# Moving two kinds of matmul operands by 32 bytes in SBUF

## The chip, the cores and the metric

The kernel runs on one core of a Trainium2 chip. The metric is the time of one execution on the device in microseconds (us), as the median of several runs. Engines are called as in the profile: PE is TensorE (matmuls), PEld its weight loads, DVE VectorE, ACT ScalarE, POOL GpSimd, SP the engine whose queue issues all transfers. A matmul has a stationary operand (128x128, loaded beforehand by an instruction of its own) and a moving operand (128 partitions by 256 or 512 columns here), and writes to PSUM.

## What is computed

Causal attention with decay, whose output goes through two feed-forward blocks. Cut to what matters:

```python
scores = (q @ k.T) / sqrt(64) * where(i >= j, gamma[h] ** (i - j), 0)   # 8 x 8 heads, 576 positions
x = (scores @ v)                                  # as 4608 tokens x 512
h = maximum(maximum(x @ w1, x @ w2), x @ w3)      # 768 wide
x = h @ w_out                                     # 512 wide
a, b = x @ w1, x @ w2                             # second block, 1024 wide
x = (a * b @ w3) @ w_out                          # 512 wide
```

The products need float32 accuracy: each operand is split into a high and a low part of the type float32r (`xh`, `xl`), and a product is made of three: high by high, low stationary by high moving, high stationary by low moving.

## The kernel before

There are five stages of matmuls, in this order of time.

- **First product** (`products`, L476), with the attention of later tokens between its groups (L335 to L402). Blocks of 512 tokens; for each of 6 row blocks `f` and 3 weights `i`, 12 matmuls of 512 columns go into one PSUM bank `ps_h`. Stationary: `w1h`, `w1l`, from the pool `w1`. Moving: `xh`, `xl`, from the pools `x0`, `x1`, `x2`. The first matmuls of all are cut in halves of 256 columns.
- **Product z** (the loop over `z_groups`, banks `ps_X`, `ps_V`, `ps_Y`), a Strassen form with 7 products a group: 4 groups of 512 columns (126 matmuls each) and one of 256. Stationary: the sums `za11h` to `zs4l`; moving: the ring `hh`, `hl`. Both from the pool `zp`.
- **Product of w3 and w_out** (`ps_w`): 192 matmuls of 512 columns. Stationary: `th`, `tl`; moving: `oh`, `ol`; both from the pool `t34`, which also has the landing tiles `raw34`.
- **Gate product** (the loop over `visits`, banks `ps_x`, `ps_v`, `ps_y`): ten visits, eight with 512 columns (168 matmuls each) and two, next to each other, with 256. Stationary: `a..`, `s..` in pieces of the pool `ws` and two of the pool `wk`. Moving: one of two operand sets in turn, `ops[0]` in the pool `op0` and `ops[1]` in the pool `op1`.
- **Last product** (`add_o`), 18 steps `s` of 84 matmuls of 256 columns. Stationary: `a11h` to `s4l`, made by `g_steps(s)` in `gpool[s % 2]`: the pool `ga` for even steps and `gb` for odd ones. Moving: tiles `k..` of the pool `ga` and pieces `w..` of the pool `ws`. The matmuls run in the order of the program; the first two products of step s + 1 (`a11`, `a12`) run ahead of the last one of step s (`a22`).

All of them are issued by two lines, L476 and L705 (`product`), so the rows of the trace are told apart by tile names. All transfers are issued by SP in program order (`load`, L100).

**Where the tiles lie.** Pools have a side. Those of the left are stacked upwards from the bottom of SBUF: the first tile lies at byte 640 of each partition, which is a multiple of 64, and all tiles ahead of the matmul operands are multiples of 256 bytes, so every operand on the left (`w1`, `x0` to `x2`, `t34`, `ws`, `wk`, `op1`, `ga`) begins at a multiple of 64. Those of the right are stacked downwards from byte 229,344, which is 64 x 3583 + 32; their tiles are multiples of 64 too, so every operand on the right (`zp`, `op0`, `gb`, and the attention's pools) begins 32 past a multiple of 64. In a pool on the right a tile that is made later lies above the earlier ones and moves the pool's start down, so that the earlier tiles move down by its size, and the later ones don't.

The remainders by 64, as (moving, stationary): first product (0, 0); z (32, 32); product of w3 and w_out (0, 0); gate product (32, 0) with `ops[0]` and (0, 0) with `ops[1]`; last product (0, 0) in even steps and (0, 32) in odd ones.

Of the kernel before, what the change touches and what calls it, by code (L numbers as in the profile page):

```python
# [9 lines left out]
F32 = mybir.dt.float32  # L10
# [12 lines left out]
P = 128  # L23
# [65 lines left out]
def tile_retention_maxout_bilinear(ctx: ExitStack, tc, a, out):  # L89
# [3 lines left out]
    def copy_r(dst, src):  # L93
        nc.scalar.activation(dst, src, AF.Copy)  # L94

    def low(eng, dst, full, hi):
        eng.tensor_tensor(dst, full, hi.bitcast(F32), ALU.subtract)  # L97

    def load(dst, src):
        nc.sync.dma_start(out=dst, in_=src)  # L100
# [14 lines left out]
        return ps_mm.tile([P, 512], F32, tag="mm", name=name)  # L115

    left = ctx.enter_context(ExitStack())
    hb_p = left.enter_context(tc.tile_pool(name="hb", bufs=4, side="left"))
    w1_p = left.enter_context(tc.tile_pool(name="w1", bufs=1, side="left"))
    x_p = {2: left.enter_context(tc.tile_pool(name="x2", bufs=1, side="left"))}  # L120
    cv_x = ctx.enter_context(ExitStack())
    x_p.update({t: cv_x.enter_context(tc.tile_pool(name=f"x{t}", bufs=1, side="left")) for t in range(2)})
    cv = cv_x.enter_context(tc.tile_pool(name="cv", bufs=2, side="left"))
    right = ctx.enter_context(ExitStack())
# [367 lines left out]
    for t in range(n_blk):  # L492
        for f in range(KF1):
            for i in range(3):
                k = T_BLK * t + 3 * f + i
                if t < EARLY:
                    split = t == 0 and 3 * f + i < HALVED
                    for e, cols in enumerate(halves if split else (whole,)):
                        name = f"{t}.{3 * f + i}" + "ab"[e] * split
# [20 lines left out]
    def splitter(pool, src, hi, lo, eng, tag, bufs):  # L520
        raw = pool.tile([P, hi.shape[-1]], F32, tag=tag, name=tag, bufs=bufs)
        load(raw, src)

        def split():
            copy_r(hi, raw)
            low(eng, lo, raw, hi)

        return split

    def open_z():  # L530
        right.close()
        cv_x.close()
        zp["ps"] = ctx.enter_context(tc.tile_pool(name="ps_2", bufs=2, space=PSUM, side="right"))
        p = zp["p"] = bx.enter_context(tc.tile_pool(name="zp", bufs=1, side="right"))
        zp["w"] = {x: [p.tile([P, KH, half], F32R, name=f"z{x}{v}") for v in "hl"] for x in AN}

    def raw_h(tag, bufs=1):
        return zp["p"].tile([P, KH, N1], F32, tag=tag, name=tag, bufs=bufs)
# [64 lines left out]

    t_last = T_BLK * (n_blk - 1)
    when(t_last, open_z)
    for c, tag in enumerate(("T3", "T2", "b21")):
        for n, step in enumerate(z_weights(c, tag)):
# [11 lines left out]
    with tc.manual_schedule():  # L619
# [88 lines left out]
        t34, w3t, wo2 = {}, {}, {}  # L708
# [4 lines left out]
            return splitter(t34["p"], flat(w3t_d[:, k, 4 * e:4 * e + 4]), *map(flat, w3t[n]), nc.vector, "raw34", 3)  # L713

        def get_wo2(k):
            wo2[k] = [t34["p"].tile([P, DM], F32R, tag=x, name=x) for x in ("oh", "ol")]
            return splitter(t34["p"], wo2_d[:, k], *wo2[k], nc.gpsimd if k % 2 else nc.vector, "raw34", 3)

# [2 lines left out]
        def prepare_34(*gets):  # L721
            for split in pending:
                split()
            pending[:] = [get(n) for get, n in gets]

        first_34 = [((get_w3t, 0), (get_wo2, 0)), ((get_w3t, 1),), ((get_w3t, 2), (get_wo2, 1)), ()]

        def open_34():
            t34["p"] = t34x.enter_context(tc.tile_pool(name="t34", bufs=2, side="left"))

        zo_p = bx.enter_context(tc.tile_pool(name="zo", bufs=1, side="right"))

# [16 lines left out]
        for j, (_, _, _, size) in enumerate(z_groups):  # L749
# [25 lines left out]
            if j == 3:  # L775
                for step in steps:
                    step()
                sx.close()
                open_34()
                steps = [lambda gets=gets: prepare_34(*gets) for gets in first_34]  # L780
# [6 lines left out]
        def operand_set(pool, tag):  # L787
            return {x: [pool.tile([P, 2, N1], F32R, name=f"{x}{v}{tag}") for v in "hl"] for x in BN}

        ops = [operand_set(o_p, 0)]  # L790
        behind = []

        def lows():
            for fn in behind:
                fn()
            behind.clear()


        def raw_z():
            return zr_p.tile([P, 2, 2, N1], F32, tag="zr", name="zr")  # L800
# [71 lines left out]
        for n in range(2 * KF2):  # L872
            k, e = divmod(n, 2)
            th, tl = w3t.pop(n)
            for m in range(4 * e, 4 * e + 4):
                if k == 0:
                    ps_w.append(bank8(f"ps_w{m}"))
                product(ps_w[m], [(th[:, m % 4], tl[:, m % 4], *wo2[k])], k == 0, k == KF2 - 1)
                if k == KF2 - 1:
                    t = w4_p.tile([P, DM], F32, tag="w4", name="w4")  # L880
                    copy_r(t, ps_w[m])
                    load(w4_d[:, m], t)
            prepare_34(*[(get_w3t, n + 3)] * (n + 3 < 2 * KF2), *[(get_wo2, k + 2)] * (e == 1 and k + 2 < KF2))
            lows()
            if steps:
                steps.pop(0)()
# [68 lines left out]
        gpool, last, gq = [None, None], {}, {}  # L955

        def temp():
            return spare_z()
# [48 lines left out]
        def g_steps(s):  # L1007

            w, ops = {}, gq.setdefault(s, {})

            def fetch():

                lows()
                r = raw_z().rearrange("p a b (c e t) -> p (a b c) e t", c=2, e=2)
                blk, e = divmod(turn[s], 2)
                load(r.rearrange("p k e t -> p k (e t)"), g_d[blk][:, :, 2 * P * e:2 * P * e + 2 * P])
                for e in range(2):
                    for kk in range(2):
                        w[f"a{e + 1}{kk + 1}"] = r[:, 4 * kk:4 * kk + 4, e]

            def split(x, eng):
                h, l = ops[x] = [gpool[s % 2].tile([P, 4, P], F32R, tag=f"{x}{v}", name=f"{x}{v}") for v in "hl"]
                src = w[x]
                copy_r(h, src)
                if s:
                    low(eng, l, src, h)
                else:
                    behind.append(lambda: low(eng, l, src, h))

            def add(dst, x, y, op, t):  # L1030
                nc.vector.tensor_tensor(t, w[x], w[y], op)
                w[dst] = t

            def tmp():
                return temp().rearrange("p (k t) -> p k t", k=4)

            def over(dst, x, y, op, to):
                lows()
                add(dst, x, y, op, w[to])

            if s == 0:
                return [fetch,
                        lambda: split("a11", nc.vector),
                        lambda: add("s1", "a21", "a22", ALU.add, tmp()),
                        lambda: over("s3", "a11", "a21", ALU.subtract, "a21"),
                        lambda: split("a12", nc.vector),
                        lambda: add("s2", "s1", "a11", ALU.subtract, tmp()),
                        lambda: split("s1", nc.vector),
                        lambda: split("s3", nc.vector),
                        lambda: over("s4", "a12", "s2", ALU.subtract, "a12"),  # L1050
                        lambda: split("s2", nc.vector),
                        lambda: split("a22", nc.vector),
                        lambda: split("s4", nc.vector)]
            return [fetch,
                    lambda: (split("a11", nc.gpsimd), add("s1", "a21", "a22", ALU.add, tmp())),
                    lambda: (split("a12", nc.vector), add("s2", "s1", "a11", ALU.subtract, tmp())),
                    lambda: (split("s1", nc.vector), add("s3", "a11", "a21", ALU.subtract, w["a21"])),
                    lambda: (split("s2", nc.gpsimd), add("s4", "a12", "s2", ALU.subtract, w["a12"])),
                    lambda: split("s3", nc.vector),
                    lambda: (split("s4", nc.vector), split("a22", nc.gpsimd))]  # L1060
# [218 lines left out]
```

## Time and profile before

| | us |
|---|---|
| median of 3 runs | 1280.26 |
| lowest and highest | 1279.84, 1280.35 |
| the profiled execution | 1279.71 |
| its span, first to last instruction | 1278.0 |
| PE busy in the span | 1270.4 |
| DVE, ACT, POOL busy | 884.6, 488.2, 311.5 |

The page of the profile gives busy times and the chain of work that ended last. A matmul's own duration (389 ns for 512 columns) is modelled to its last write and overlaps the next, so the pace is read from the distance between starts: the length of a stretch divided by the number of matmuls that start in it. The granted clock is 1.00 of 2.4 GHz in every stretch shown.

### The profile page before, as it was taken

The numbers are of one execution on the slowest core, as the hardware profiler recorded it, in microseconds if no ns is written. First come the engines' busy times: TensorE is split into PE (matmuls) and PEld (weight loads), VectorE is DVE, ScalarE is ACT, GpSimd is POOL, SyncE is SP. The second block draws the span as 40 slices with busy tenths as digits, with TensorE's granted clock in tenths as the row PEclk, the third lists the DMA queues.
The fourth block names the chain that finished last, engine by engine and source line by source line (L and its number), as shares of the span: only waits on it lengthen the run. The fifth ranks groups of instructions, "written<-read, shape, count | busy, mean of one in ns | idle before, by whom it ended". The sixth has DMA issues, their size and how long they took to land.

```text
span 1278.0 us, 23000 instructions
## 1 busy us (share of the span) xinstructions
PE 1270.4 (99%) x8904; PEld 1088.6 (85%) x8904; DVE 884.6 (69%) x1256; ACT 488.2 (38%) x873; POOL 311.5 (24%) x259
## 2 busy tenths in 40 slices
PE   8999999999999999999999999999999999999999
PEld 6888888888888888888889788888988888999998
DVE  5985666666666765467897547775766577888885
ACT  3550122222222222225554444443433344455553
POOL 2111211111111110000000324553345352344443
DMA  9935788788888994525544641424133323445542
GB/s 215 249 100 123 147 216 200 186 206 194 225 190 169 185 208 121 180 84 198 198 157 144 219 166 70 140 77 158 63 110 117 132 74 124 156 156 161 170 151 100
DMA packets 323797, 199.34 MB, mean 156 GB/s; under 512 B 241636, under 2 KB 279270, under 8 KB 323688
## 3 DMA queue, kind: packets, MB, share of 16 engines
q1 hardware_dynamic: 323688, 197.87, 55.8%
q8 instruction: 70, 1.15, 0.4%
q14 instruction: 39, 0.32, 0.1%
HBM read 131.76 MB, written 66.06 MB: 155 GB/s over the span
## 4 chain that ended last, share of the span: by engine, by line
PE 98%; DMA 1%; DVE 0%; ACT 0%; issue 0%; SPq 0%; POOL 0%; ACTq 0%; POOLq 0%
PE ps_h L476 35%; PE ps_x L705 24%; PE ps_y L705 12%; PE ps_v L705 6%; PE ps_X L705 6%; PE ps_Y L705 3%; PE sc L359 3%; PE o L374 3%; PE ps_w L705 2%; PE ps_V L705 1%; PE st L394 1%; PE o L381 1%; DMA raw<-w3t_d 1%; PE kp L335 0%; PE warm L260 0%; PE qp L335 0%
## 5 line engine op out<-in xcount | busy, mean ns | idle before, releaser
L476 PE MATMUL ps_h<-xh,w1h 128*128 128x512 f32 (+1 forms) x664 | 257.2, 389 | 0.0
L476 PE MATMUL ps_h<-xh,w1l 128*128 128x512 f32 (+1 forms) x664 | 254.1, 384 | 0.0
L476 PE MATMUL ps_h<-xl,w1h 128*128 128x512 f32 (+1 forms) x664 | 174.1, 384 | 0.0
L476 PEld LDWEIGHTS ps_h<-xh,w1h 128*128 128x128 f32 x664 | 124.7, 188 | 27.6 <-issue 2.1
L476 PEld LDWEIGHTS ps_h<-xh,w1l 128*128 128x128 f32 x664 | 124.8, 188 | 24.0
L476 PEld LDWEIGHTS ps_h<-xl,w1h 128*128 128x128 f32 x664 | 123.1, 188 | 24.7
L486 DVE TENSOR_TENSOR hb<-ps_h,hb 128x512 f32<-128x512 f32 (+1 forms) x110 | 74.3, 677 | 96.8 <-PE ps_h L476 85.5
L1133 POOL TENSOR_TENSOR c<-c 128x512 f32<-128x512 f32 (+1 forms) x60 | 83.5, 1392 | 181.9 <-DVE c L1125 127.9
L1120 ACT ACTIVATE snap<-ps_x 128x512 f32<-128x512 f32 (+1 forms) x100 | 55.5, 555 | 182.0 <-PE ps_x L705 169.6
L345 POOL TENSOR_TENSOR q<-q,tables 128x512 f32<-128x512 f32 (+1 forms) x31 | 31.3, 1009 | 278.7 <-DMA q<-in_q_dram 207.0
L94 ACT ACTIVATE hb<-ps_h 128x512 f32<-128x512 f32 (+1 forms) x56 | 32.5, 580 | 141.7 <-PE ps_h L476 141.7
L160 ACT ACTIVATE e<-raw 128x512 f32<-128x512 f32 x64 | 42.8, 669 | 105.3 <-DMA raw<-in_moe_w_dram 70.9
L94 ACT ACTIVATE xh<-o 128x512 fp32r<-128x512 f32 (+1 forms) x40 | 22.2, 555 | 119.9 <-PE o L381 84.3
L97 POOL TENSOR_TENSOR ol<-raw,oh 128x512 fp32r<-128x512 f32 x4 | 5.7, 1432 | 239.7 <-DVE tl L97 218.7
L348 POOL TENSOR_TENSOR v<-v,tables 128x512 f32<-128x512 f32 x40 | 43.5, 1089 | 59.3 <-DMA v<-in_v_dram 59.3
L366 DVE TENSOR_TENSOR p<-sc,mask 128x512 f32<-128x512 f32 (+1 forms) x80 | 48.1, 627 | 12.9 <-PE sc L359 12.8
L1125 DVE TENSOR_TENSOR c<-ps_x,snap 128x512 f32<-128x512 f32 (+1 forms) x40 | 25.2, 637 | 43.2 <-PE ps_x L705 31.1
L166 DVE CUSTOM_DVE_ANT_0 m<-m,r 128x1024 uint16<-128x1024 uint16 x64 | 48.6, 759 | 7.5 <-ACT r L161 0.5
L1125 DVE TENSOR_TENSOR c<-ps_v,snap 128x512 f32<-128x512 f32 (+1 forms) x40 | 25.1, 635 | 37.8 <-PE ps_v L705 20.9
L705 PE MATMUL ps_x<-t4h,a 128*128 128x512 f32 (+1 forms) x160 | 45.9, 370 | 0.3 <-DVE a L97 0.3
L705 PE MATMUL ps_x<-b11h,a 128*128 128x512 f32 (+1 forms) x160 | 45.8, 371 | 0.0
L169 DVE SCALAR_TENSOR_TENSOR m<-raw,m 128x512 int32<-128x512 int32 x64 | 45.5, 715 | 0.3
(296 smaller groups left out, 3281.0 us busy)
## 6 DMA issues: line engine op xcount, KB each, us to landing
zr<-g_d SPq DMA_DIRECT2D x18, 1024.0 KB, 6.1
raw<-in_moe_w_dram SPq DMA_DIRECT2D x34, 512.0 KB, 6.1
g_d<-c SPq DMA_DIRECT2D x64, 256.0 KB, 2.0
zr<-z_d SPq DMA_DIRECT2D x28, 512.0 KB, 5.3
h_d<-hb SPq DMA_DIRECT2D x54, 256.0 KB, 3.2
b<-h_d SPq DMA_DIRECT2D x16, 768.0 KB, 6.2
out_dram<-ob SPq DMA_DIRECT2D x35, 256.0 KB, 2.1
v<-in_v_dram SPq DMA_DIRECT2D x32, 256.0 KB, 4.4
```

The lines of the kernel that those rows point to most:

```text
L94: nc.scalar.activation(dst, src, AF.Copy)
L160: nc.scalar.activation(z["e"], raw[:, :, 1].bitcast(F32), AF.Copy, scale=2.0 ** -112)
L166: nc.vector.tensor_tensor(z["m"], z["m"], z["r"], ALU.add)
L169: nc.vector.scalar_tensor_tensor(z["m"], z["hi"], -0x80000000, z["m"], ALU.bitwise_and, ALU.bitwise_or)
L348: nc.gpsimd.tensor_tensor(z["v"], z["v"], vd.unsqueeze(2).to_broadcast([P, H, D]), ALU.mult)
L366: nc.vector.tensor_tensor(z[g][:c, :, :c], z["sc"][g][:c, :, :c], mask[:c, :c].unsqueeze(1).to_broadcast([c, G, c]), ALU.mult)
L476: nc.tensor.matmul(ps[:, cols], l, r, start=n == 0, stop=n == len(mms) - 1)
L486: nc.vector.tensor_tensor(hb, ps[:, cols], hb, ALU.max)
L705: nc.tensor.matmul(ps, l, r, start=start and j == 0, stop=stop and j == len(mms) - 1, skip_group_check=again)
L1120: nc.scalar.activation(t, ps[:, :size], AF.Copy)
L1125: nc.vector.tensor_tensor(r, ps[:, :size], t, ALU.add)
L1133: nc.gpsimd.tensor_tensor(x, x, y, ALU.mult)
```

## The change

A helper `skew` makes a tile of 32 bytes per partition (8 float32) that nothing reads or writes. It is called in seven places:

```diff
     left = ctx.enter_context(ExitStack())
+    def skew(pool, n=0):
+        pool.tile([P, 8], F32, name=f"skew{n}", bufs=1)
+
+    skew(ctx.enter_context(tc.tile_pool(name="edge", bufs=1, side="right")))
     hb_p = left.enter_context(tc.tile_pool(name="hb", bufs=4, side="left"))
     w1_p = left.enter_context(tc.tile_pool(name="w1", bufs=1, side="left"))
+    skew(w1_p)
     x_p = {2: left.enter_context(tc.tile_pool(name="x2", bufs=1, side="left"))}
+    skew(x_p[2])
...
         zp["w"] = {x: [p.tile([P, KH, half], F32R, name=f"z{x}{v}") for v in "hl"] for x in AN}
+        skew(p)
...
         def get_wo2(k):
+            if k == 0:
+                skew(t34["p"], 1)
             wo2[k] = [t34["p"].tile([P, DM], F32R, tag=x, name=x) for x in ("oh", "ol")]
...
             t34["p"] = t34x.enter_context(tc.tile_pool(name="t34", bufs=2, side="left"))
+            skew(t34["p"])
...
             def split(x, eng):
+                if not ops and s in (0, 3):
+                    skew(gpool[s % 2])
                 h, l = ops[x] = [gpool[s % 2].tile([P, 4, P], F32R, tag=f"{x}{v}", name=f"{x}{v}") for v in "hl"]
```

The pool `edge` lies at the right-hand end for the whole kernel and moves everything on the right down by 32 bytes. The first tile of `w1` moves its weights up by 32; the one in `x2` brings `xh` and `xl` of all three pools back to a multiple of 64. In `zp` the tile comes after the sums and before the ring, so the sums move by 32 more than the ring. In `t34` one tile moves `th`, `tl` and `raw34`, and a second one `oh` and `ol` back. In `ga` (s = 0) the tile comes after the moving tiles `k..` and ahead of the stationary ones; in `gb` (s = 3) it is the last tile of its pool and moves all others down.

The remainders by 64 afterwards: first product, z, product of w3 and w_out, and both kinds of steps of the last product (0, 32); gate product (0, 0) with both sets. The attention's operands move by 32 together.

## Rows read from the trace of the kernel before

**Rows 1.** The page: busy time by engine, and the chain's shares by engine.
```profile
PE 1270.4 (99%) x8904; PEld 1088.6 (85%) x8904; DVE 884.6 (69%) x1256; ACT 488.2 (38%) x873; POOL 311.5 (24%) x259
...
PE 98%; DMA 1%; DVE 0%; ACT 0%; issue 0%; SPq 0%; POOL 0%; ACTq 0%; POOLq 0%
```

**Rows 2.** Waits of PE, longest first (total, times, longest).
```profile
PE sc L359 <- DVE qt L342: 1.9, 2, 1.0
```

**Rows 3.** Busy time by stretch; columns as in the first line.
```profile
core 0: us, PE busy (x) PEld busy (x) DVE busy (x) ACT busy (x) POOL busy (x), PEclk, DMA share, GB/s
513.82:568.21 54.39, 54.39 (x241) 45.06 (x240) 29.25 (x52) 15.86 (x31) 0.00 (x0) 1.00 0.44 150
570.48:684.76 114.28, 114.28 (x505) 94.59 (x504) 96.79 (x89) 61.77 (x71) 0.00 (x0) 1.00 0.52 174
684.77:699.87 15.10, 15.10 (x127) 15.10 (x126) 10.11 (x16) 9.33 (x17) 0.00 (x0) 1.00 0.38 124
...
745.23:784.43 39.20, 39.20 (x169) 31.54 (x168) 22.15 (x26) 16.67 (x30) 17.43 (x12) 1.00 0.34 121
784.44:822.55 38.11, 38.11 (x169) 31.54 (x168) 29.14 (x36) 18.23 (x34) 18.93 (x12) 1.00 0.32 111
901.82:929.41 27.59, 27.59 (x232) 27.59 (x231) 19.77 (x39) 12.92 (x31) 7.39 (x9) 1.00 0.17 59
1018.08:1056.19 38.11, 38.11 (x169) 31.54 (x168) 24.87 (x30) 15.54 (x28) 17.58 (x12) 1.00 0.28 91
1056.20:1095.40 39.20, 39.20 (x169) 31.54 (x168) 30.30 (x42) 18.26 (x34) 9.93 (x6) 1.00 0.38 127
1110.00:1278.00 168.00, 164.96 (x1391) 164.76 (x1390) 137.24 (x178) 84.66 (x178) 70.43 (x49) 1.00 0.47 150
```

**Rows 4.** Starts of matmuls of the last product: start, duration, engine, line, what.
```profile
1138.19 0.29 PE L705 MATMUL ps_y<-kt,s1h 128*128 128x256 f32 x1
...
1143.94 0.28 PE L705 MATMUL ps_x<-kb,a11h 128*128 128x256 f32 x1
...
1148.20 0.28 PE L705 MATMUL ps_y<-kt,s1h 128*128 128x256 f32 x1
...
1153.83 0.28 PE L705 MATMUL ps_x<-kb,a11h 128*128 128x256 f32 x1
```

**Rows 5.** Groups by form: count, busy us and mean ns of one, idle before.
```profile
L476 PE MATMUL ps_h<-xh,w1h 128*128 128x512 f32 x632 | 248.7, 394 | 0.0
L476 PE MATMUL ps_h<-xh,w1l 128*128 128x512 f32 x632 | 246.2, 389 | 0.0
L476 PE MATMUL ps_h<-xl,w1h 128*128 128x512 f32 x632 | 169.0, 389 | 0.0
...
L705 PE MATMUL ps_w<-oh,th 128*128 128x512 f32 x64 | 25.1, 393 | 0.4 <-ACT th L94 0.3
...
L476 PEld LDWEIGHTS ps_h<-xh,w1l 128*128 128x128 f32 x664 | 124.8, 188 | 24.0
```

**Rows 6.** The chain that ended last, from 700 us: start, us, what.
```profile
700.08 0.40 ACT zo L742
...
701.25 4.62 DMA raw<-w3t_d
...
707.36 6.54 DMA raw<-w3t_d
...
715.41 29.97 PE ps_w L705 x131
```

**Rows 7.** Starts of product z's first matmuls.
```profile
570.48 0.40 PE L705 MATMUL ps_X<-hh,za11h 128*128 128x512 f32 x1
...
572.57 0.39 PE L705 MATMUL ps_X<-hh,za11h 128*128 128x512 f32 x1
```

## The prediction, written before the changed kernel ran

> **What bounds the kernel now.** I read the page's list of engines and its chain first [rows 1]. TensorE is busy for 1270.4 of 1278.0 us and carries 98% of the chain that ended last. The list of waits has no wait of TensorE over 1.9 us in total [rows 2]. So the time is the number of matmuls times the distance from the start of one to the start of the next, and a change that waits for nothing and computes nothing can act only on that distance. The next view is the table of stretches [rows 3], where the number of weight loads counts the matmuls, since each has one; the stretches are cut at starts of matmuls.
>
> At the granted clock of 1.00, which is the level of 2.4 GHz, 512 columns take 213.3 ns. No stretch reaches that. I set each beside the byte addresses of its operands, worked out from the pools as the kernel's section tells; (0, 32) means moving operand at a multiple of 64 bytes, stationary one 32 past.
> - First product: 54.39 us for 240 is 226.6 ns. (0, 0).
> - Product z: 114.28 us for 504 is 226.7 ns. (32, 32).
> - Gate visits with the operand set on the left (784.44 and 1018.08): 38.11 us for 168 is 226.8 ns. (0, 0).
> - Gate visits with the set on the right (745.23 and 1056.20): 39.20 us for 168 is 233.3 ns. (32, 0). Same instructions, same counts; only the side of the moving operands differs.
> - 256 columns take 106.7 ns at this clock. The half of z: 15.10 us for 126 is 119.8 ns, (32, 32). A run inside the half visit: 27.59 us for 230 (its counters include one or two that reach in) is 120.0 ns, (32, 0).
> - Last product, read from starts [rows 4]: 48 matmuls from 1138.19 to 1143.94 are 119.8 ns (operands of an even step, on the left, (0, 0)); the same 48 from 1148.20 to 1153.83 are 117.3 ns (odd step, on the right, (0, 32)).
>
> So equal remainders cost 13.3 ns over the columns at either width; (32, 0) costs 20.0 at 512 columns and 13.3 at 256; (0, 32) costs 10.6 at 256. **At 512 columns (0, 32) is in no row, and it is what the change makes of most of the kernel.**
>
> **The change part by part.** It adds no instruction, wait or buffer; each padding is an unused tile of 32 bytes per partition. Queues, orders and DMAs stay.
>
> *Gate product.* The padding at the right-hand edge takes the right set's moving operands from 32 past to a multiple of 64, and leaves the stationary ones: (32, 0) becomes (0, 0). Price from the rows of the other set: 39.20 - 38.11 = 1.09 us a visit, four whole visits (two of each are shown, the other two read alike): **-4.4 us**. The half visit goes from 120.0 to 119.8 ns: nothing.
>
> *Last product.* Even steps go from (0, 0) to (0, 32), odd ones keep (0, 32). 18 steps of 84 matmuls, half of them even: 756 x 2.5 ns = **-1.9 us**. DVE is busy for 137 of 168 us there and TensorE waits some 3 us in this stage, most of it at the very end, so I count the gain in full.
>
> *First product, z, and the product of w3 and w_out.* 3 x 632 = 1896 matmuls of 512 columns [rows 5], then 504, then 192 (3 x 64), 2592 in all, go to (0, 32). Bounds for one: the nearest rows below are the 13.3 ns over the columns, all of which could go at most (213.3, -34.6 us); above, the worst row at this width, 233.3 ns (+6.6 each, +17.1 us). I take the saving that the same remainders show at 256 columns, 119.8 - 117.3 = 2.5 ns, because it is the only row with them, and because a weight load is the same 128 columns at either width: 2592 x 2.5 = **-6.5 us**. The 126 and 96 matmuls of half width in z and in the opening: **-0.6 us**. Not all arrives: between 700.05 and 715.4 us the chain leaves TensorE and goes through ACT, two landings of w3t_d of 4.62 and 6.54 us and DVE [rows 6], so the gain of the some 60 matmuls of that stretch is lost (0.2 us); the opening's waits take perhaps as much again.
>
> *Cover.* The other engines and the transfers keep their times and get a little less room. The tightest stage is z, with DVE busy for 96.8 of 114.3 us; it becomes some 113. DVE's waits there are for earlier work, and even a saving of 6.6 ns each (111 us) stays above 96.8. If that cover were gone, at most z's own saving (1.3 us) would be lost. Landing tiles on the right move from 32 past to multiples of 64; those of w3t_d and wo2_d move the other way. No landing but those of [rows 6] is on the chain, and a tenth on these two would be 1.1 us.
>
> The sum: -4.4 - 1.9 - 6.5 - 0.6 + 0.4 = -13.0 us. The profiled execution took 1279.71 us (span 1278.0), 0.55 below the median of 1280.26. So 1267.2, about **1267 us**.
>
> **The rivals.**
> - *Settled or not (slower).* Where the remainders are equal, a run begins unevenly and then settles: z's first nine distances, 570.48 to 572.57, have a mean of 232.2 ns, after which they stay at 226.7 [rows 3, 7]. All settled rows are 13.3 ns over their columns at both widths. (0, 32) doesn't come to that value (10.6 over 48 matmuls at 256 columns), nor does (32, 0) at 512 (20.0 over 168), so I take these two for unsettled to the end. (32, 0) costs 233.3 at 512 and 120.0 at 256: 113.3 for 256 columns more, not the 106.7 of settled runs. If not settling is what costs, (0, 32) at 512 columns is 117.3 + 113.3 = 230.6 ns: 2592 x 3.9 = +10.1, and the time is 1280.3 - 4.4 - 1.9 - 0.6 + 10.1 = 1283.5. It decides from a price above 226.7 + 2.7 = 229.4 ns, where the certain 6.9 us are used up. For it: nine uneven distances at the very width that matters. Against: the unsettled runs at 512 all had moving operands off the multiple or came out of a pause, and the one unsettled row with them on it is the cheapest row there is.
> - *A whole step of 16 columns.* 233.3 - 226.7 is 6.6 ns, which is 16 columns or 64 bytes at this clock. With moving operands 32 past, shifting the stationary ones by 32 is worth just that (233.3 against z's 226.7). If it is worth the same with moving operands at 0, one takes 220.1 ns: 2592 x 6.6 = 17.1 in place of 6.5, which gives 1256.6. Against it: at 256 columns the same shift is worth 2.5 in one pair of rows and nothing in the other.
> - *Only at 256 columns.* The saving of the last product belongs to matmuls shorter than their load (188 ns in the row of loads [rows 5]); at 512 nothing changes. -4.4 - 1.9 - 0.6 gives 1273.4.
> - *A wider distance counts.* Odd steps now have stationary minus moving at 96 modulo 128, afterwards 32, which is what the right set's gate visits have now (120.0 at 256). Then the last product loses 756 x 2.7 = 2.0 us in the odd steps and gains none; with the unsettled price at 512 and no gain in the gate product: +10.1 + 2.0 gives 1292.
> - *Addresses don't matter.* The change does nothing, 1280.3, if the 1.09 us between the gate visits have another cause, such as the work that runs beside them. Against: visits of a set agree within 0.01 us whatever runs beside them.
> The Trainium skill stands with this last rival: "TensorE: Matmul & The Clock Gate", Step-by-step (1), says that matmul and weight load have separate read ports into SBUF, so that loading the next weights takes no bandwidth from the running matmul; "SBUF — State Buffer", Specifications, counts lines of 16 bytes, to which every operand here is aligned before and after. By both the time would stay. The trace disagrees with the first as far as the two kinds of gate visit go (39.20 against 38.11 us).
>
> **How the numbers follow.** Forecast 0.33; a whole step 0.18; only at 256 columns 0.14; settled or not 0.22; wider distance 0.08; no effect 0.05. The measurement of this kernel can tell about 0.2%, or 2.6 us, from no change. Faster: 0.33 + 0.18 + 0.14 = 0.65. Same: 0.05, and 0.04 of the unsettled case, whose price may come out near 229.4. Slower: 0.26. The forecast's own range is 1263 to 1271. The range that should hold 8 in 10 reaches from 1256 to 1285; it leaves out the wider distance and the lower half of the whole step (0.17).
>
> **What would show it.** In the profile after: gate visits all at 38.1 us (right: the sum's first term; at 39.2: address isn't it). Even and odd steps of the last product both at 117.3 (at 119.8 both: wider distance). The decisive one is the first product's 240 matmuls: 53.8 us is my price, 52.8 the whole step, 55.3 the unsettled one, 54.4 no effect at this width. z's 504 should read 113.0 us. I am wrong if those rows are above 54.4 and 114.3, whatever the gate product gives.

## The result, and the profile after

The changed kernel takes 1288.94 us in the median, the kernel before 1279.65; the ratio is 1.0067, with a 95% interval of 1.0056 to 1.0079. One of the changed kernel's six executions took 1431.52 us at a mean granted clock of 0.82, and the ratio leaves it out. The change makes the kernel slower, by some 9 us, where 13 us less were forecast. The two profiled executions, 1289.01 us after and 1279.71 before, stand for this: 9.3 us, and it is these two that are taken apart here.

The page after: busy time by engine, and the chain's shares by engine.

```profile
PE 1278.9 (99%) x8904; PEld 1084.6 (84%) x8904; DVE 890.8 (69%) x1256; ACT 488.6 (38%) x873; POOL 312.7 (24%) x259
...
PE 96%; DMA 2%; DVE 1%; ACT 0%; issue 0%; SPq 0%; ACTq 0%; DVEq 0%
```

Same counts as in [rows 1], TensorE still busy for 99% of the span, the chain still TensorE's. TensorE is busy 8.5 us longer with the same 8904 matmuls. Of the waits from 34 us to the start of the last product, here with the wait's total, count and longest, none reaches half a microsecond:

```profile
PE ps_x L712 <- DVE a L97: 0.3, 1, 0.3
PE o L380 <- issue: 0.3, 1, 0.3
PE ps_w L712 <- ACT th L94: 0.2, 1, 0.2
```

So no wait came in; the matmuls start further apart. The table of stretches after, cut at the starts of the same matmuls as in [rows 3] (columns: stretch and its length; busy us and instructions of PE, PEld, DVE, ACT and POOL; granted clock, DMA share, GB/s):

```profile
521.80:577.79 55.99, 55.99 (x241) 44.99 (x240) 29.33 (x52) 15.97 (x31) 0.00 (x0) 1.00 0.43 145
580.13:697.72 117.59, 117.59 (x505) 94.47 (x504) 96.96 (x89) 61.95 (x71) 0.00 (x0) 1.00 0.51 169
697.73:712.82 15.09, 14.95 (x128) 14.77 (x126) 10.11 (x16) 9.19 (x17) 0.00 (x0) 1.00 0.37 120
759.03:797.47 38.44, 38.44 (x169) 31.55 (x168) 22.12 (x26) 16.63 (x30) 17.49 (x12) 1.00 0.34 122
797.48:835.58 38.10, 38.10 (x169) 31.54 (x168) 29.24 (x36) 18.23 (x34) 18.97 (x12) 1.00 0.31 111
914.08:941.16 27.08, 27.08 (x232) 27.08 (x231) 19.80 (x39) 12.91 (x31) 7.41 (x9) 1.00 0.18 61
1066.63:1105.10 38.47, 38.47 (x169) 31.55 (x168) 30.39 (x42) 18.25 (x34) 9.96 (x6) 1.00 0.39 129
```

The first product's 240 matmuls went from 54.39 to 55.99 us, which is 233.3 ns each in place of 226.6; z's 504 from 114.28 to 117.59 us, 233.3 in place of 226.7. The granted clock reads 1.00 in all these rows; what that reading is worth for the trace before stands in the last section. The gate visits with the right-hand set fell from 39.20 to 38.44 us, not to 38.1; the half visit's 230 matmuls fell from 27.59 to 27.08.

In the last product, starts of the same matmuls as in [rows 4] (start, duration, engine, line, what):

```profile
1147.76 0.28 PE L712 MATMUL ps_y<-kt,s1h 128*128 128x256 f32 x1
...
1153.44 0.28 PE L712 MATMUL ps_x<-kb,a11h 128*128 128x256 f32 x1
...
1157.70 0.28 PE L712 MATMUL ps_y<-kt,s1h 128*128 128x256 f32 x1
...
1163.38 0.28 PE L712 MATMUL ps_x<-kb,a11h 128*128 128x256 f32 x1
```

48 matmuls take 5.68 us in an even step and in an odd one: 118.3 ns, where it was 119.8 and 117.3. The even steps won and the odd ones lost.

From starts of the same matmuls in both traces the 9.3 us come together thus:

| stage | before, us | after, us | difference |
|---|---|---|---|
| opening, to the 401st matmul | 35.99 | 33.71 | -2.3 |
| rest of the opening, attention and first product | 534.49 | 546.42 | +11.9 |
| z, 512 columns | 114.29 | 117.60 | +3.3 |
| z, its half | 15.11 | 15.09 | 0.0 |
| product of w3 and w_out | 45.35 | 46.21 | +0.9 |
| gate product | 350.18 | 346.08 | -4.1 |
| last product, to its last matmul | 179.27 | 178.85 | -0.4 |

The opening's -2.3 us go with the clock that the two executions had there, as the last section tells, and are not shown to come from the change. Without them the change costs 11.6 us here.

### The profile page after: what moved, and what is told of

It reads as the page before. It is cut to its first block, busy times and chain, and to the rows that moved or that the text cites. A ratio compares the mean times of both kernels' runs of the same rounds, so it can differ in the third digit from the quotient of the medians.

```text
span 1287.3 us, 23000 instructions
## 1 busy us (share of the span) xinstructions
PE 1278.9 (99%) x8904; PEld 1084.6 (84%) x8904; DVE 890.8 (69%) x1256; ACT 488.6 (38%) x873; POOL 312.7 (24%) x259
## 4 chain that ended last, share of the span: by engine, by line
PE 96%; DMA 2%; DVE 1%; ACT 0%; issue 0%; SPq 0%; ACTq 0%; DVEq 0%
PE ps_h L482 35%; PE ps_x L712 23%; PE ps_y L712 11%; PE ps_v L712 6%; PE ps_X L712 6%; PE ps_Y L712 3%; PE sc L365 3%; PE o L380 3%; PE ps_w L712 2%; PE ps_V L712 1%; PE st L400 1%; PE o L387 1%; DMA raw<-w3t_d 1%; PE kp L341 0%; DVE p L372 0%
## 5 line engine op out<-in xcount | busy, mean ns | idle before, releaser
L482 PE MATMUL ps_h<-xh,w1h 128*128 128x512 f32 (+1 forms) x664 | 260.6, 394 | 0.0
L482 PE MATMUL ps_h<-xh,w1l 128*128 128x512 f32 (+1 forms) x664 | 257.3, 389 | 0.0
L482 PE MATMUL ps_h<-xl,w1h 128*128 128x512 f32 (+1 forms) x664 | 177.9, 389 | 0.0
L97 POOL TENSOR_TENSOR ol<-raw,oh 128x512 fp32r<-128x512 f32 x4 | 5.3, 1326 | 250.0 <-DVE tl L97 228.9
L372 DVE TENSOR_TENSOR p<-sc,mask 128x512 f32<-128x512 f32 (+1 forms) x80 | 48.1, 626 | 13.5 <-PE sc L365 13.4
L1137 DVE TENSOR_TENSOR c<-ps_x,snap 128x512 f32<-128x512 f32 (+1 forms) x40 | 25.2, 637 | 40.4 <-PE ps_x L712 17.1
```

Source lines behind the costliest of these rows:

```text
L372: nc.vector.tensor_tensor(z[g][:c, :, :c], z["sc"][g][:c, :, :c], mask[:c, :c].unsqueeze(1).to_broadcast([c, G, c]), ALU.mult)
L482: nc.tensor.matmul(ps[:, cols], l, r, start=n == 0, stop=n == len(mms) - 1)
L1137: nc.vector.tensor_tensor(r, ps[:, :size], t, ALU.add)
```

## The experiments

Eight kernels follow, one of them with three traces. In what follows the *distance* of a matmul is the byte address of its stationary operand less that of its moving one in a partition, modulo 256; why 256, and not 64 as in the prediction, is what the first four show. Addresses come from the pools, as in the kernel's section. All but the extra edits use the changed kernel's paddings with sizes of their own, a size of zero leaving the padding out:

```diff
+    PAD = {...}                # bytes, by place
+    def skew(pool, name):
+        if PAD.get(name):
+            pool.tile([P, PAD[name] // 4], F32, name=f"skew_{name}", bufs=1)
```

The places are `edge` (right-hand edge), `w1`, `x2`, `z` and `ta`, `tb` (the two of `t34`), `ga`, `gb`, as in the change, and `op0`, `op1`, which are new: ahead of the tiles in the gate product's two sets.

**The moving operands' part alone.**

```diff
+    PAD = {'edge': 32}
```

> Only the 32 bytes at the right-hand edge; no other padding. Distance below is stationary start minus moving start, modulo 256 bytes. Product z keeps distance 0, with both operands 192 past a multiple of 256 (before: 224); the right-hand gate visits get distance 192, odd steps of the last product 64. Theory S (a run settles to the cheap pace only at distance 0): z stays at 226.7 ns a matmul; the right-hand gate visits read 229.0 as in the changed kernel (38.47 us a visit), so -2.9 us for four visits, the half visits -1.1 us; time about 1276, give or take 2 for the odd steps, whose distance 64 no run has shown. Rival M (a moving operand at 192 past a multiple of 256 is dear in itself): z rises to 229 to 233.3 (+1.2 to +3.3 us). If the opening's 2.2 us come from tiles on the right landing at multiples of 64, they show here too and the time is about 1274; if they were chance, they don't.

It took 1276.84 us, ratio 0.9971 (0.9959 to 0.9982): faster than before. In the table of stretches, first product, z, a right-hand gate visit and the half visit:

```profile
513.89:568.28 54.39, 54.39 (x241) 45.05 (x240) 29.24 (x52) 15.97 (x31) 0.00 (x0) 1.00 0.45 150
570.56:685.56 115.00, 114.52 (x505) 94.52 (x504) 96.77 (x89) 61.79 (x71) 0.00 (x0) 1.00 0.53 173
746.32:784.78 38.46, 38.46 (x169) 31.55 (x168) 22.18 (x26) 16.68 (x30) 17.46 (x12) 1.00 0.34 123
901.41:928.50 27.09, 27.09 (x233) 27.09 (x231) 19.81 (x39) 12.92 (x31) 7.41 (x9) 1.00 0.18 61
```

z's operands moved together, from remainder 224 by 256 to 192, and z's matmuls still start every 226.9 ns (one longer distance, a wait for VectorE, left out). So where the moving operand begins is not what counts. The gate visit shows 228.9 ns and not 226.8, although both operands are now at multiples of 64: its distance is 192. All that the change gained in the gate product comes from this part, and elsewhere it costs under 1 us a stage (0.7 in z, by the wait).

**The stationary operands' part alone.**

```diff
+    PAD = {'w1': 32, 'x2': 32, 'z': 32, 'ta': 32, 'tb': 32, 'ga': 32}
```

> The paddings on the left, in z and in the pools of the other three stages, without the one at the right-hand edge: first product, z and the product of w3 and w_out get distance 224, the gate product and odd steps of the last one stay as before, even steps get 32. Theory S: first product, z and w3-w_out cost 233.3 ns at 512 columns as in the changed kernel, +15.8 us in all, even steps 118.3 in place of 119.9 (-1.2): about 1294. Rival M (dear because the moving operand lies at 192): the first product, moved to 192, costs 233.3, but z's ring lies at 224 here and stays at 226.7: about 1291. Rival R (what counts is the edge: landing tiles and the gate product slow the changed kernel): about 1267 to 1280.

It took 1294.53 us, ratio 1.0113 (1.0091 to 1.0135). First product, z, and a right-hand gate visit:

```profile
523.08:579.07 55.99, 55.99 (x241) 44.98 (x240) 29.33 (x52) 15.95 (x31) 0.00 (x0) 1.00 0.44 145
581.41:699.36 117.95, 117.83 (x505) 94.38 (x504) 96.94 (x89) 61.88 (x71) 0.00 (x0) 1.00 0.50 169
760.22:799.42 39.20, 39.20 (x169) 31.54 (x168) 22.06 (x26) 16.63 (x30) 17.42 (x12) 1.00 0.33 120
```

The whole loss is here. z, whose moving operands lie 32 past a multiple of 64 in this kernel and at one in the changed kernel, takes 233.5 ns here (one longer distance left out) and 233.3 there: again not the place, but that the two operands no longer lie at the same one. One part of the expectation failed. The odd steps of the last product, at the addresses they had before, took 118.8 ns and not 117.4, which is 1.1 us; why is not known.

**Other distances, in two kernels.**

```diff
+    PAD = {'x2': 224, 'z': 192, 'op0': 224, 'op1': 160, 'ga': 64, 'gb': 224}
```

> Paddings of other sizes, to read the pace at distances that no row has: first product 32, z 64, gate product 128 (right, half visits too) and 96 (left), even steps of the last product 64, odd ones 128; w3-w_out stays at 0. Theory S: every one of the 512-column rows lies above 226.8 ns, at 228 to 235 (the first product's 240 matmuls take 54.8 to 56.4 us, z's 504 take 114.9 to 118.5), and the time is 1285 to 1300. Rival R64 (only the remainder by 64 counts, as in the prediction): z at 64 and the right-hand visits at 128 have equal remainders and take 226.7; only 32 and 96 are dearer. Rival W (a distance other than 0 can be cheaper than 0 at 512 columns): one of the four rows lies under 226.7.

```diff
+    PAD = {'z': 256, 'op0': 128, 'op1': 192, 'ga': 192, 'gb': 128}
```

> More distances: z at 256 (that is 0 by 256, but not by 512), gate product 32 (right, half visits too) and 64 (left), even steps of the last product 192, odd ones 224; first product and w3-w_out as before. Theory S with a period of 256: z stays at 226.7 (114.3 us for 504); with a period of 512 it rises to 229 or more (over 115.4 us). The gate visits give a second reading of 32 and 64 beside the first product and z of the run before: equal to them within 0.5 ns if distance alone decides, different if the place of the moving operand matters too. At 256 columns 192 and 224 read 116.6 and 116.9, as in the half visits and in the halves of the first product of the changed kernel: the last product takes some 4 us less than before.

They took 1293.98 and 1283.89 us, one execution each. The first two rows are the first kernel's, z at distance 64: the groups of 512 columns, then the half. The third is the second kernel's, z's groups of 512 columns at distance 256.

```profile
581.27:698.86 117.59, 117.59 (x505) 94.25 (x504) 97.02 (x89) 61.97 (x71) 0.00 (x0) 1.00 0.51 169
698.87:713.18 14.31, 14.31 (x127) 14.30 (x126) 9.97 (x16) 9.03 (x17) 0.00 (x0) 1.00 0.38 126
...
572.08:686.49 114.41, 114.41 (x505) 94.52 (x504) 96.76 (x89) 61.79 (x71) 0.00 (x0) 1.00 0.52 174
```

At one and the same distance, 512 columns take 233.3 ns, the dear price, and 256 columns 113.6 (14.31 / 126), the cheapest anywhere. What a distance gives at one width says nothing for the other. In the second kernel z had its operands 256 bytes further apart than before, and kept 227.0 ns; the stationary operand 64 bytes past the moving one cost 233.3 there too, in the gate visits on the left (39.17 us). In the first kernel distance 128 cost 233.3 as well, in the gate visits on the right. So the distance repeats with 256, and not with 64 or 128. At 256 columns the second kernel missed its expectation: distances 192 and 224 gave some 117.8 ns in the last product and not 116.6 and 116.9, so this stage won 1.1 us and not 4. All prices stand in the table at the end.

**Each width at its best distance.** If that is right, the right-hand side must move by 96 bytes and not by 32 (distance 0 in the gate product's right-hand visits, z unchanged), and the last product wants 64 in all its steps.

```diff
+    PAD = {'edge': 96, 'ga': 64, 'gb': 192}
```

> One pad of 96 bytes on the right side and one in each of the two pools of the last product (64 and 192 bytes): every product of 512 columns has its moving and its stationary operand at the same remainder by 256, and the last product has its stationary operand 64 bytes past that in every step; all else as before. Theory D (the pace hangs on the distance of the two operands' starts, counted in 256 bytes): the gate's four whole right visits go from 39.2 to 38.1 us (226.8 ns a matmul, -4.4 us), the gate's left visits, first product, z and w3w_out stay at 226.8, the last product goes to 114.0 ns in even steps (756 x (119.8 - 114.0) = -4.4 us) and in odd ones (756 x (117.3 - 114.0) = -2.5 us); sum -11.3 us, 1268 to 1269 us. If the odd steps of the run with the right-hand pad alone (the same distance, 117.7 ns) are what 64 bytes give when all steps have them, the last product saves 1.3 us and the sum is -5.7 us, 1274 us. Rival A (remainders by 64 bytes are what counts, so 64 bytes past is the same as no distance): gate -4.4 us, last product at 119.8 ns in all steps, +1.9 us, 1277 us. Rival of my prediction, that 32 bytes past is the better place: not touched here.

It took 1267.97 us, ratio 0.9906 (0.9884 to 0.9927), the fastest median of all kernels here, and 21 us below the changed kernel. Right-hand gate visit, and 48 matmuls of an even and of an odd step of the last product:

```profile
745.55:783.62 38.07, 38.07 (x169) 31.53 (x168) 22.14 (x26) 16.63 (x30) 17.37 (x12) 1.00 0.35 124
...
1132.83:1138.26 5.43, 5.43 (x50) 5.43 (x49) 4.45 (x5) 3.17 (x7) 2.66 (x3) 1.00 0.55 183
1142.35:1147.78 5.43, 5.43 (x50) 5.43 (x49) 4.44 (x5) 3.17 (x7) 2.65 (x3) 1.00 0.64 181
```

38.07 us is 226.6 ns, and 5.44 us (from start to start) is 113.3 ns in both kinds of step. In the gate visit the operands' starts differ by 256 modulo 512, a second reading that 256 counts as 0. The gate product took 4.7 us less than before and the last product 7.1; the opening took 2.2 less, and 2.5 were lost in the other stages, z's wait of 0.7 among them. The rival by which only the remainders by 64 count is out: it gave 1277 us. One execution of six took 1275.36 us; the next kernel shows what may be most of it, but this execution has no trace.

**And the slices of half width too.**

```diff
+    def col(size):
+        return 48 if size < N1 else 0
-            hh, hl = ... [:, :, :size]
+            hh, hl = ... [:, :, col(size):col(size) + size]
```

and the same slice, `col(size):col(size) + size`, for the gate product's sets.

> The run before it in this list, and besides the slices of 256 columns of z's half group and of the gate's two half visits begin 192 bytes later in their tiles, so that the stationary operand is 64 bytes past the moving one by 256 there too. Theory D: z's 126 matmuls of 256 columns go from 119.8 to 113.5 ns (-0.8 us, if the stall that the changed kernel had there does not return), the half visits' 336 from 119.9 to 113.5 ns (-2.1 us): 2.9 us below the run without it, 1265 to 1266 us in all. Rival A: nothing, the same time as the run without it. Rival W (the half visits wait for VectorE's and GpSimd's sums and not for TensorE): the pace falls and the visit does not, gain under 1 us.

> The kernel of e6_paired_halves once more, for a trace of its second kind of execution: four of its six took 1272.7 to 1273.0 us and the profiled one 1265.3. Theory U (the pace at a distance of 64 bytes settles in one of two ways, as the 113.6 ns of e5's last product and the 117.7 ns of e1's odd steps hint): in an execution of 1272.7 us the last product takes 118.5 ns a matmul in place of 113.6 (1512 x 4.9 ns = 7.4 us) and all else is alike. Theory T (a transfer that comes late in the opening or between z and the gate): the last product stays at 113.6 ns, and the 7.4 us stand in one or two gaps ahead of it. In an execution near 1265 us neither can be seen.

> As the run before it in this list: the same kernel, a further look, with the same two theories. Theory U: 118.5 ns in the last product where the time is 1272.7 us, 113.6 where it is 1265. Theory T: 113.6 ns in both, and the difference in gaps.

Three executions of this kernel have a trace: 1265.32, 1268.26 and 1271.13 us. The median of six timed ones is 1272.69, with four of the six between 1272.67 and 1273.02; so no gain over the kernel without this edit is shown. z's half takes 14.83 us (117.8 ns, forecast 113.5) and the half visits 116.7 ns (forecast 113.5); the gain in these two is 0.3 and 1.1 us, in all three traces alike. Between the fastest of the three and the slowest, what differs is the last product. (The 2.9 us of the middle one lie in three places of the attention instead, where TensorE waited for GpSimd, VectorE and ScalarE, the longest for 1.1 us.) The execution of 1265.32 us, 48 matmuls each from its first step, its second, the turn from its third to its fourth, and late:

```profile
1090.90:1096.54 5.64, 5.64 (x50) 5.64 (x49) 3.35 (x6) 2.32 (x5) 1.29 (x1) 1.00 0.59 197
1100.74:1106.20 5.46, 5.46 (x50) 5.46 (x49) 5.27 (x7) 3.96 (x10) 3.00 (x2) 1.00 0.42 136
1117.60:1123.03 5.43, 5.43 (x50) 5.43 (x49) 4.73 (x8) 3.32 (x8) 3.04 (x2) 1.00 0.30 100
1236.38:1241.81 5.43, 5.43 (x50) 5.43 (x49) 5.13 (x7) 2.46 (x6) 1.94 (x2) 1.00 0.75 220
```

The same matmuls in the execution of 1271.13 us:

```profile
1090.83:1096.47 5.64, 5.64 (x50) 5.64 (x49) 3.34 (x6) 2.33 (x5) 1.29 (x1) 1.00 0.58 194
1100.70:1106.13 5.43, 5.43 (x50) 5.43 (x49) 5.24 (x7) 3.93 (x10) 3.00 (x2) 1.00 0.42 131
1117.82:1123.46 5.64, 5.64 (x50) 5.64 (x49) 4.68 (x7) 3.21 (x8) 3.04 (x2) 1.00 0.30 100
1241.25:1246.89 5.64, 5.64 (x50) 5.64 (x49) 5.24 (x7) 2.60 (x6) 1.88 (x2) 1.00 0.72 207
```

Both begin at 117.8 ns a matmul (5.65 / 48) and go to 113.3 in the second step (the 5.46 us hold a few longer distances). At the end of the second step TensorE pauses for VectorE, for some 0.5 us from one start to the next, and out of that pause the first execution comes with 113.3 ns and the second with 117.8. Each keeps its pace through all later steps, the same instructions at the same addresses. The last product takes 172.2 us in the one and 178.1 in the other, and the gate product 344.4 in both. The same last product stands in four more traces (the middle execution, the kernel before this one and the two that follow), and all four took 172.2 us. So two settled paces are shown, with 117.8 ns for the dear one and not the 118.5 I had worked out from 7.4 us; the executions of 1272.7 us themselves have no trace. What decides which pace comes out of the pause was not found out; it was 483 ns long in the one dear trace and 495 to 512 in the five others.

**Finer distances.** The ring of z's moving operands was shifted by 4 to 48 bytes, with tiles 64 bytes longer, so that each group of z runs through four distances.

```diff
+    PAD = {'edge': 96, 'z': 224, 'ga': 64, 'gb': 192}
+    OFF = (16, 48, 28, 36, 4)
-            hh, hl = ... zp["p"].tile([P, KH, N1], ...)[:, :, :size]
+            hh, hl = ... zp["p"].tile([P, KH * N1 + 16], ...)[:, OFF[j] // 4:OFF[j] // 4 + KH * N1] ...
```

> The first of this list, but with z's moving operands set off in steps of 16 and 4 bytes: distances 16, 48, 80, 112, 144, 176, 208, 240 in the first two of its four groups, 4, 60, 68, 124, 132, 188, 196, 252 in the other two. Theory D as the runs so far have it (226.8 ns at distance 0, 229.0 at 192, 233.3 at the other multiples of 32): all of the new distances lie at 233.3 ns or between 226.8 and 233.3, none below 226.7; z then takes 504 x (229 to 233.3 - 226.8) = 1 to 3.3 us more. If a distance below 32 bytes gives another whole step of 16 columns, some of these matmuls start every 220.0 ns. Rival A (remainders by 64): distances that differ by 64 have the same pace.

It took 1268.35 us, in one execution. The distances in it came out as expected, since the longer tiles shift one another. z's groups of 512 columns took 117.06 us, 232.3 ns a matmul, against 226.7 at distance 0; the means of the sixteen distances lie between 228.7 and 237.7, four of them above the 233.3 that was expected as the highest. No distance gives less than 226.7. More can't be read from it, because a stream of mixed distances doesn't show each matmul's own price, as the last kernel tells: distances that differ by 64 do have means within 3 ns of each other, but just these were mixed in one group.

**One operand of three apart.** The low halves of z's stationary operands 32 bytes further, nothing else.

```diff
+    PAD = {'edge': 96, 'ga': 64, 'gb': 192}
-        zp["w"] = {x: [p.tile([P, KH, half], F32R, name=f"z{x}{v}") for v in "hl"] for x in AN}
+        his = [p.tile([P, KH, half], F32R, name=f"z{x}h") for x in AN]
+        p.tile([P, 8], F32, name="skew_low", bufs=1)
+        zp["w"] = {x: [h, p.tile([P, KH, half], F32R, name=f"z{x}l")] for x, h in zip(AN, his)}
```

> The kernel of e5_paired with one thing more: of z's stationary operands the low halves start 32 bytes later, so that of each three matmuls (high weights, low weights, high weights) the second has its own operand at distance 32 and the first has it in the weights that are loaded beside it for the next one; all else at distance 0. Theory O (a matmul is slowed by the distance of its own stationary operand): the second of each three starts the next after 233.3 ns, the others after 226.7. Theory N (it is slowed by the distance of the weights that are loaded while it streams): the first of each three takes 233.3, the others 226.7. Either way z takes 168 x 6.6 ns = 1.1 us more than in e5_paired, 1269 us in all. Theory S (the distance sets a state of the whole stream, not a matmul's own time): all three lie together, at 226.7 or at 233.3 (+3.3 us), 1268 or 1271 us.

It took 1271.70 us, in one execution, and z's 504 matmuls 117.60 us, as much as in the changed kernel, where all are apart. The row of z, and starts in its middle, of which `zs3l` is the operand that lies apart:

```profile
570.98:688.57 117.59, 117.59 (x505) 94.46 (x504) 96.97 (x89) 61.86 (x71) 0.00 (x0) 1.00 0.51 169
...
589.88 0.40 PE L718 MATMUL ps_X<-hh,zs3h 128*128 128x512 f32 x1
590.12 0.39 PE L718 MATMUL ps_X<-hh,zs3l 128*128 128x512 f32 x1
590.34 0.40 PE L718 MATMUL ps_X<-hl,zs3h 128*128 128x512 f32 x1
590.58 0.40 PE L718 MATMUL ps_X<-hh,zs3h 128*128 128x512 f32 x1
```

Over all of z the three distances between starts are 239.4, 228.1 and 232.5 ns: the longest stands where the weights 32 bytes apart are the next to be loaded, but all three are above 226.7, and their sum is 700.0, three times 233.3. So one operand of three costs the stream as much as all three. The theories that price each matmul by itself at 6.6 ns, by its own weights or by the next ones, would have had a third of the loss; the theory of a state of the whole stream has the sum right, but not that all three distances are alike.

## Why the prediction was wrong

**The step that failed** is the price of the pair (0, 32) at 512 columns, 2592 x 2.5 ns. I took the 2.5 ns that the last product showed at 256 columns [rows 4] for the same saving at 512. It is no saving at all there: 233.3 against 226.7 ns is 2592 x 6.6 = +17.1 us, and 16.1 arrived (11.9 + 3.3 + 0.9). That is the upper bound that the prediction named for an operand pair no row showed, the price of the other unequal pair at this width [rows 3]. The nearest row was the one of the same width, not the one of the same remainders; the kernel with z at distance 64, 233.3 ns at one width and 113.6 at the other, shows how little the widths have in common.

Behind it stands a second error, in how the rows were grouped. Remainders by 64 put the odd steps of the last product and the changed first product in one class, (0, 32). By 256 the odd steps had a distance of 96 before, and the changed first product has 224: not even the same pair. The other terms, point by point:

- *Gate product*, forecast -4.4, measured -4.1, for the wrong reason. The whole right-hand visits gave only -3.0 (four times 0.74), because both operands at multiples of 64 is distance 192 here, 228.9 ns, and not 0; with 96 bytes in place of 32 the forecast's 38.1 us is met (38.07). The other 1.1 us came from the half visits, for which I had counted nothing: 192 is better than 160 at 256 columns.
- *Last product*, forecast -1.9, measured -0.4. The even steps went to 118.3 ns and not to 117.3; the odd ones, which I said keep their pair, went from distance 96 to 32 and lost 1.0 ns.
- *Halves*, forecast -0.6: z's half measured 0.0. Its matmuls did come closer, from 119.9 to 116.7 ns, but two longer distances that were not there before took 0.4 us back.
- *No wait, no new work*: right but for those two distances. The list of waits after shows nothing over 0.3 us from 34 us to the last product, and z's VectorE, at 97 of 117.6 us, stayed covered.
- *The opening* gave 2.3 us that no step had. That is luck as far as the forecast goes: it hides a fifth of the loss; see the last section.

**The rivals.** "Settled or not" named the right sign and the right kind of thing, that two unequal operands keep a stream from the 13.3 ns over its columns, and its test said 55.3 us for the 240 matmuls, where 55.99 came. Its price, 230.6 ns, was worked out across the widths as well; with 233.3 in its place its time is 1283.5 + 2592 x 2.7 ns = 1290.5, against 1289.0. "A wider distance counts" was right that 64 is too small a period, with 128 in place of 256; it gave 1292. "A whole step of 16 columns" saw the step, 6.6 ns, with the wrong sign. "Only at 256 columns" and "addresses don't matter" are out.

The range, 1256 to 1285, ended 4 us short. The upper bound of the unknown price, +6.6 ns a matmul, gives the same 1290.5 us with the prediction's other terms (1280.3 - 6.9 + 17.1). The prediction named this bound, and then ended its range by the slower rival's own price.

The Trainium skill, "TensorE: Matmul & The Clock Gate", Step-by-step (1), has separate read ports for weights and moving operand, so that loading takes no bandwidth from a running matmul. No run here shows the ports. What the runs show does not agree with it as a statement on time: the same matmuls of 512 columns start every 226.7 or 233.3 ns by nothing but the distance of the two operands. What in the chip makes this distance count is open.

## What to carry over

Where TensorE is the bound and a weight load runs beside every matmul, look at the byte distance of the two operands modulo 256, for each width of its own: here 0 was best for 512 columns of float32r and 64 for 256 (at 113.3 ns, but it can also run at 117.8), and at 512 columns a single operand of three out of place cost as much as all three. No run here has another type. Count addresses by the longest period that the rows allow, and where a width has no row for the case at hand, take the ends of that width's own rows and keep them in the range. Before a pad is put everywhere, try it on each side alone: one half of this change was worth -3.6 us and the other +14.

## What the runs showed of the hardware

Mean distance from start to start, in ns, by the distance of the operands in bytes modulo 256 (float32r, 128x128 weights, granted clock 1.00 in the rows; waits left out; worked out from all starts of a stage, so mixed of settled and unsettled parts):

| distance | 0 | 32 | 64 | 96 | 128 | 160 | 192 | 224 |
|---|---|---|---|---|---|---|---|---|
| 512 columns | 226.8 | 233.3 | 233.3 | 234.3 | 233.3 | 233.4 | 229.0 | 233.3 |
| 256 columns | 119.9 | 118.4 | 113.5 to 117.8 | 117.4 to 118.8 | 118.4 | 120.0 | 116.6 to 117.9 | 116.7 to 117.7 |

At 512 columns equal places are best, and at 256 they are among the worst. The prices at 512 columns were the same within 0.5 ns in every kernel that had them. At 256 columns the distance alone does not set the pace: where a range stands, different stages or kernels gave different values. At distance 64 there are two paces for one kernel, and a pause can change one into the other, which makes 5.9 us here.

The opening differs by TensorE's clock. Its 401st matmul started at 36.0 us before, and between 35.8 and 36.2 in the two kernels with one half of the change and in the second of the two with other distances; in all others, the changed kernel too, between 33.7 and 34.6. The first attention scores, the same instructions in every kernel, show what it is. Each pair of rows is of the same matmuls: the scores in the kernel with each width at its best distance and in the changed kernel, then a longer stretch in the changed kernel and in the kernel before.

```profile
8.70 1.10 PE L368 MATMUL sc<-qt,kt 64*64 64x128 f32 x32 [0.95 <-DVE qt L351]
8.10 1.99 PE L365 MATMUL sc<-qt,kt 64*64 64x128 f32 x32 [0.95 <-DVE qt L348]
...
8.00:11.00 3.00, 2.90 (x48) 2.55 (x48) 0.78 (x2) 0.00 (x0) 0.73 (x1) 0.50 0.96 239
9.70:12.70 3.00, 2.89 (x48) 2.55 (x48) 0.78 (x2) 0.00 (x0) 1.04 (x1) 1.00 1.00 236
```

From the first start to the last, the 32 matmuls take 0.83 us in the first kernel, at a recorded granted clock of 1.00 (the level of 2.4 GHz), and 1.57 us in the changed kernel, at a recorded 0.50 (1.2 GHz), to which it had fallen at 7.6 us; from 6 to 8 us TensorE was busy there for 0.83 us. The kernel before takes 1.57 us too, although its row reads 1.00. Its trace holds no record of the clock at all, and a stretch without a record reads 1.00; by its own pace it ran these matmuls at the lower level. The three other traces with a late 401st matmul have their first record, of 1.00, at 13.4 to 13.9 us, all others at 4.1 to 6.4 us. When the clock rises differs between executions of one kernel: it is at 4.4, 6.1 and 5.9 us in the three traces of the kernel with the slices of half width. The right-hand padding does not decide it either: the opening is late with that padding alone and early in the first kernel with other distances, which lacks it. So the opening's 2.3 us are not shown to be the work of the addresses; the kernel before has only one trace here. For the later stages its reading of 1.00 is borne out, as the same distances give the same 226.7 ns in the traces whose records do cover them.
